# The last block product of a two-level second product: its third column block moved to the end, in two halves

## The chip, the cores and the metric

The kernel runs on one core of one Trainium2 chip. The core has a matrix engine (TensorE, "PE" in the profile, with its weight loads as "PEld"), a vector engine (VectorE, DVE), an activation engine (ScalarE, ACT), a general engine (GpSimd, POOL) and a queue processor for transfers (SyncE, SP). ACT and POOL can issue transfers too. Products are summed in PSUM banks, which VectorE or ScalarE then read; everything else lives in SBUF.

The metric is device microseconds of one execution. A difference of about 0.3% (4.06 us) is what a measurement of this kernel can tell from none.

## The reference

Attention with normalised queries and keys, then a feed-forward block with a squared ReLU. Batch 8, 12 heads, 448 tokens, head size 64; the attention output is laid out as x of 3584 tokens x 768.

```
q_n, k_n = rmsnorm(q, g_q), rmsnorm(k, g_k)
attn = softmax(q_n @ k_n.T / sqrt(64))
x = (attn @ v) as (3584, 768)
h = x @ w_in                 # 768 -> 2048
g = max(h, 0) ** 2
out = g @ w_out              # 2048 -> 768, float32
```

The change touches only the last lines of the work: the product with w_out for the last two batches.

## The kernel before

**Stages.** The tokens are worked through in four spans of two batches (2 x 448 tokens). Attention of the next span runs beside the second product of this one, so that TensorE has matmuls to do while softmax work waits. Both products are block products of the Strassen-Winograd kind: the operands are split in 2 x 2 blocks, seven products of sums of blocks take the place of eight, and adds on VectorE, ScalarE and POOL put the output blocks together. The sums of weight blocks are formed once, early, and kept in device memory (`w2s` for the second product).

**The last span.** Nothing is left to run beside the second product of the last span, so it is done by `last_product` (L1144 to L1318), which divides each of the seven block products again. They are called A11, A12, S2, S1, S3, A22, S4 and are taken in that order by the loop at L1210; `o` counts them and `end` is true for the last, S4. One block product is 384 output columns (three column blocks of 128, numbered m = 0, 1, 2) x 448 tokens, summed over 1024 channels (eight chunks of 128).

Column blocks 0 and 1 are the inner 2 x 2: two column blocks, two halves of the tokens (224 each), two halves of the sum (four chunks each). `run` (L1204) makes one inner product of four matmuls of 128 x 128 by 128 x 224; the trace shows each float32 matmul as two rows, so eight rows. Seven of these follow each other on TensorE: pa (a11 b11), pb (s2 t2), pc (s1 t1), pd (s3 t3), then pa, pd and pc are added to (a12 b21, a22 t4, s4 b22). The inner sums s1 to s4 come from POOL (`add_weights`, L1174) and t1 to t4 from VectorE (`add_g`, L1186); both are formed one block product ahead.

The third column block has no partner. `third` (L1229) computes it directly: eight matmuls of 128 x 448 tokens into one PSUM bank (16 rows in the trace, L1233), then one add of 448 columns on VectorE (L1239). In the order of the program it stands between the first inner product (pa) and the second (pb) of every block product, S4's too.

**PSUM banks.** `bank` gives out two banks in turn ("m" and "n"). Each block product takes two: one for the third column block, one for pc. pa, pb and pd have banks of their own.

**How results leave.** Four of the seven block products finish output blocks (`leaves`). `deliver` (L1137) turns one column block of 128 x 448 on VectorE (a 32 x 32 transpose, L1139) into a buffer of five (`osb`) and sends it with four transfers of 32 rows each (L1142); each piece written to the output is 128 bytes. For most, the transfers all go to SP's queue; blocks 0 and 1 are kept in `late` and delivered at the start of the next block product. For S4 the transfers alternate between SP's queue and ACT's (`queues`, L1225), and blocks 0 and 1 are sent in halves of 224 tokens as they come ready: `send(1, latter)` at L1291, `send(0, former)` at L1301, `send(1, former)` at L1306, `send(0, latter)` at L1311. The third block is sent whole at L1270.

So S4 delivers five times: one whole block (4 transfers of 56 KB) and four halves (16 transfers of 28 KB).

**Order.** The order of instructions on each engine is the order of the program text (the schedule is manual). The layer that builds the program adds waits on semaphores. Transfers issued by SP and ACT share eight completion semaphores, given out in turn in an order that the building layer estimates over both queues. Before an issue, its queue waits until the transfer that had the semaphore before has landed; the queue stands still meanwhile.

**The end.** The whole of this lies in one side of an `If` (L1456; the other side is a kernel for large scores, not run here). Behind the last instruction each engine branches to the common end (L1486), where SP waits for the semaphores of all transfers and the engines meet.

Of the kernel before, what the change touches and what calls it, by code (L numbers as in the profile page):

```python
# [387 lines left out]
def attention_then_ffn_bounded(  # L388
# [35 lines left out]
    nc = tc.nc  # L424

    B, H, S, D = q.shape
# [8 lines left out]
    HC = NPAIR // 2  # L435
    HF = NFC // 2
# [23 lines left out]
    def bank(name, n=None):  # L460

        turn[0] += n is None
        return ps_m.tile([P, S], F32, tag="mn"[turn[0] % 2 if n is None else n], name=name)
# [673 lines left out]
    def deliver(work, span, ct, col, t, queues=(nc.sync,), part=slice(0, S // 32), kept=2):  # L1137
        osb = work.tile([P, S // 32, 32], F32, tag="osb", name="osb", bufs=kept)[:, part]
        nc.vector.transpose(osb.rearrange("p g n -> p (g n)"), ct[:, part.start * 32:part.stop * 32])  # L1139
        for i in range(0, P, 32):  # L1140
            queue = queues[i // 32 % len(queues)]
            queue.dma_start(rows[2 * span + t, :, part, col * P + i:col * P + i + 32], osb[i:i + 32])  # L1142

    def last_product(pool):  # L1144

        rhs_of = {A11: gT[:, 0:HF, 0:S], S2: gC[:, 1], S1: gC[:, 0], S3: gT[:, 0:HF, S:2 * S],
                  A12: gT[:, HF:, 0:S], A22: gC[:, 2], S4: gT[:, HF:, S:2 * S]}
        order = (A11, A12, S2, S1, S3, A22, S4)
        HK, HS = HF // 2, S // 2
# [7 lines left out]
        ts = [[t[:, n * NT2:(n + 1) * NT2].rearrange("p (c n) -> p c n", c=HK) for n in range(4)] for t in (cf, xf)]  # L1157
        dead = [gT[:, f, 0:S] for f in range(HF)] + [gC[:, 1, f] for f in range(HF)]
        late = []
        former, latter = slice(0, HS // 32), slice(HS // 32, S // 32)  # L1160
        sub, add = ALU.subtract, ALU.add

        def weights_of(o, m, k):
            return sets[o % 2].rearrange("p (k c n) -> p k c n", k=2, c=HK)[:, k, :, m * P:(m + 1) * P]

        def sums_of(o):
            return [t.rearrange("p (c n) -> p c n", c=HK) for t in left[o % 2]]
# [6 lines left out]
        def add_weights(o):  # L1174
            if o == len(order):
                return
            s1, s2, s3, s4 = sums_of(o)
            (a11, a12), (a21, a22) = [[weights_of(o, m, k) for k in range(2)] for m in range(2)]
            for dst, x, y, op in ((s1, a21, a22, add), (s2, s1, a11, sub), (s3, a11, a21, sub), (s4, a12, s2, sub)):
                nc.gpsimd.tensor_tensor(dst, x, y, op)  # L1180

        def parts_of(o):
            rhs = rhs_of[order[o]]
            return [[rhs[:, k * HK:(k + 1) * HK, t * HS:(t + 1) * HS] for t in range(2)] for k in range(2)]

        def add_g(o, n):  # L1186
            if o == len(order):
                return
            (b11, b12), (b21, b22) = parts_of(o)
            t1, t2, t3, t4 = ts[o % 2]  # L1190
            dst, x, y = ((t1, b12, b11), (t2, b22, t1), (t3, b22, b12), (t4, b21, t2))[n]
            nc.vector.tensor_tensor(dst, x, y, sub)

        def small_of(name):
            return work.tile([P, HS], F32, tag=name, name=name, bufs=1)
# [8 lines left out]
        def run(ps, lhs, rhs, first=True):  # L1204
            for c in range(HK):
                nc.tensor.matmul(ps, lhs[:, c], rhs[:, c], start=first and c == 0, stop=c == HK - 1,  # L1206
                                 skip_group_check=not first)

        turn[0] += 1
        for o, i in enumerate(order):  # L1210
            end = o + 1 == len(order)
            (b11, b12), (b21, b22) = parts_of(o)
            (a11, a12), (a21, a22) = [[weights_of(o, m, k) for k in range(2)] for m in range(2)]
            s1, s2, s3, s4 = sums_of(o)
            t1, t2, t3, t4 = ts[o % 2]

            into = {A11: [(None, p1s)], A12: [(p1s, None)], S2: [(p1s, p1s)], S1: [(p1s, ys)],
                    S3: [(ys, None), (p1s, p1s)], A22: [(p1s, None)], S4: [(ys, None)]}[i]
            leaves = any(dst is None for _, dst in into)
            into = [(base, dst or homes[i]) for base, dst in into]  # L1220
            at = ((HC if i in (S3, A22) else 0), 1 if i in (S3, S4) else 0)

            def send(m, part=slice(0, S // 32)):
                deliver(work, NSPAN - 1, into[0][1][m], m + at[0], at[1],
                        (nc.sync, nc.scalar) if end else (nc.sync,), part, 5)  # L1225

            both = len(into) > 1

            def third():  # L1229
                m = HC - 1  # L1230
                ps = bank("ps")
                for c in range(HF):
                    nc.tensor.matmul(ps, weights_of(o, m, c // HK)[:, c % HK], rhs_of[i][:, c],  # L1233
                                     start=c == 0, stop=c == HF - 1)
                for base, dst in into:
                    if base is None:
                        nc.scalar.copy(dst[m], ps)
                    else:
                        nc.vector.tensor_tensor(dst[m], base[m], ps, add)  # L1239

            def meet(m, t, left, ps):

                part = slice(t * HS, (t + 1) * HS)
                dst = blocks[m] if both else into[0][1][m]
                nc.vector.tensor_tensor(dst[:, part], left, ps, add)

            def based(m, t, x, name):
                base = into[0][0]
                if both or base is None:
                    return x  # L1250
                y = small_of(name)
                nc.gpsimd.tensor_tensor(y, x, base[m][:, t * HS:(t + 1) * HS], add)
                return y

            def settle(m):
                for base, dst in into if both else ():
                    nc.gpsimd.tensor_tensor(dst[m], base[m], blocks[m], add)

            pa = ps_s.tile([P, 2, 512], F32, tag="s", name="pa")[:, 0, 0:HS]
            run(pa, a11, b11)  # L1260
            p1 = small_of("p1i")
            nc.scalar.copy(p1, pa)
            for n in range(3 if o else 0):
                add_g(o + 1, n)
            for args in late:
                deliver(*args)
            late[:] = []
            third()
            if leaves:
                send(HC - 1)  # L1270
            pb = ps_o.tile([P, S], F32, tag="o", name="pb")[:, 0:HS]
            run(pb, s2, t2)
            z, y = small_of("zi"), small_of("yi")
            nc.vector.tensor_tensor(z, p1, pb, add)
            z21, z12 = based(1, 0, z, "za"), based(0, 1, z, "zb")
            pc = bank("pc")[:, 0:HS]
            run(pc, s1, t1)
            nc.vector.tensor_tensor(y, z, pc, add)
            if o:
                add_g(o + 1, 3)  # L1280
            pd = ps_o.tile([P, S], F32, tag="t", name="pd")[:, 0:HS]
            run(pd, s3, t3)
            add_weights(o + 1)
            if both or into[0][0] is None:
                meet(1, 1, y, pd)
            else:
                meet(1, 1, into[0][0][1][:, HS:S], pd)
                x = into[0][1][1][:, HS:S]
                (nc.vector if end else nc.gpsimd).tensor_tensor(x, x, y, add)
            if end:  # L1290
                send(1, latter)  # L1291
            if o == 0:
                for n in range(4):
                    add_g(1, n)
            run(pa, a12, b21, False)
            if both or into[0][0] is None:
                nc.scalar.copy((blocks if both else into[0][1])[0][:, 0:HS], pa)
            else:
                meet(0, 0, into[0][0][0][:, 0:HS], pa)
            if end:  # L1300
                send(0, former)  # L1301
            run(pd, a22, t4, False)
            meet(1, 0, z21, pd)
            settle(1)
            if end:
                send(1, former)  # L1306
            run(pc, s4, b22, False)
            meet(0, 1, z12, pc)
            settle(0)
            if end:  # L1310
                send(0, latter)  # L1311
            elif leaves:
                for m in (1, 0):
                    late.append((work, NSPAN - 1, into[0][1][m], m + at[0], at[1], (nc.sync,), slice(0, S // 32), 5))
            if o == 0:
                combine(HF - 1)
            load_set(o + 2)
# [173 lines left out]
```

## Time and profile before

| what | us |
|---|---|
| median of 3 runs (1354.04 to 1357.3) | 1354.34 |
| the profiled execution, its own time | 1357.6 |
| its span, first to last instruction | 1355.3 |
| TensorE busy | 1332.5 |
| VectorE, ScalarE, POOL busy | 873.7, 432.1, 619.8 |
| S4's block product on TensorE, from its second product (pb) to its end | 1336.3 to 1345.5 |
| S4's third column block, first row to the next product's first | 6.0 |
| last transpose on VectorE ends | 1346.4 |
| last output transfer issued (SP) | 1350.5 |

The profiled execution took 2.3 us more than its span, and 3.3 us more than the median of the runs. Times in the text are counted from the start of its span.

How to read the views: a row of the timeline has its start, its length, engine, line, operation, what is written and read, shape and count, and in brackets how long the engine was idle before and what ended that. A "q" behind an engine's name means its queue processor: an issue of a transfer, a wait, a branch. A row of the waits has who waited for whom, the sum, the number and the longest. The landing of a transfer is when its semaphore has counted all of its 16 parts.

### The profile page before, as it was taken

To read this page: it belongs to the slowest core of one execution; us is meant where nothing else is said; L and a number is where in the kernel's file an instruction comes from. 1 tells how busy PE (TensorE), PEld (TensorE's weight loads), DVE (VectorE), ACT (ScalarE), POOL (GpSimd) and SP (SyncE) were. 2 spreads that over 40 slices of the span, in tenths; PEclk is the share of its full clock that TensorE was granted. 3 is DMA by queue.
4 is the path that set the end of the run, shared out by engine and by line. 5 is a ranking of instruction groups with operands and counts; after the bars stand their busy time and mean duration, and the time that the engine had idled before them with its cause. 6 is when DMAs were issued, how large, how long until landed. Compare 5 with 4: busy or idle time off the path is not lost.

```text
span 1355.3 us, 17250 instructions
## 1 busy us (share of the span) xinstructions
PE 1332.5 (98%) x5770; PEld 669.6 (49%) x5770; DVE 873.7 (64%) x1537; ACT 432.1 (32%) x681; POOL 619.8 (46%) x504
## 2 busy tenths in 40 slices
PE   8999999999999999999999999999999999999997
PEld 3333445444444455444444455544444445556886
DVE  5999788599987433568777623457878733336552
ACT  7887466533342011233333111223333201111000
POOL 5667533456664122646555212446556412322452
PEclk8999999999999999999999999999999999999999
DMA  9777999655685433345675433345655444431333
GB/s 240 196 244 199 296 364 329 190 126 111 128 160 127 101 87 88 101 111 116 142 147 121 115 96 87 92 109 126 134 120 124 111 100 136 132 88 47 114 106 53
DMA packets 413878, 190.15 MB, mean 140 GB/s; under 512 B 282452, under 2 KB 408788, under 8 KB 413780
## 3 DMA queue, kind: packets, MB, share of 16 engines
q1 hardware_dynamic: 406196, 180.21, 51.8%
q0 software_dynamic: 4736, 8.40, 2.4%
q8 instruction: 48, 0.79, 0.3%
q10 hardware_dynamic: 2848, 0.34, 0.2%
q14 instruction: 50, 0.41, 0.1%
HBM read 155.72 MB, written 33.16 MB: 139 GB/s over the span
## 4 chain that ended last, share of the span: by engine, by line
PE 90%; DVE 5%; ACT 3%; issue 1%; DMA 0%; POOL 0%; DVEq 0%; ACTq 0%
PE ps L1106 29%; PE pd L1068 10%; PE pa L1068 10%; PE pc L1068 10%; PE sc L785 7%; PE pav L862 7%; PE pb L1068 5%; PE ps L1233 3%; PE pd L1206 2%; PE pc L1206 2%; PE pa L1206 2%; ACT gT L797 1%; PE sc L793 1%; DVE gT L810 1%; PE pb L1206 1%
## 5 line engine op out<-in xcount | busy, mean ns | idle before, releaser
L1106 PE MATMUL ps<-gT,sw 128*128 128x448 f32 x576 | 225.8, 543 | 0.0
L1044 POOL TENSOR_TENSOR gT<-gT 128x448 f32<-128x448 f32 x96 | 94.2, 983 | 285.2 <-ACT gT L1040 285.2
L750 POOL TENSOR_TENSOR half<-half,mhalf 128x28 f32<-128x28 f32 x36 | 175.1, 4863 | 74.4 <-DVE half L749 71.2
L1106 PE MATMUL ps<-gC,sw 128*128 128x448 f32 x432 | 170.1, 543 | 0.0
L1106 PEld LDWEIGHTS ps<-gT,sw 128*128 128x128 f32 x576 | 107.5, 190 | 113.9 <-issue 110.4
L1068 PE MATMUL pa<-xT,sw 128*128 128x448 f32 x384 | 155.0, 540 | 0.6 <-ACT p L1072 0.6
L1040 ACT ACTIVATE gT<-gT 128x448 f32<-128x448 f32 x96 | 55.4, 577 | 313.5 <-DVE gT L1083 313.5
L1106 PEld LDWEIGHTS ps<-gC,sw 128*128 128x128 f32 x432 | 80.6, 190 | 86.3 <-issue 84.1
L787 ACT ACTIVATE pr<-sc 128x896 f32<-128x896 f32 x87 | 77.5, 915 | 122.5 <-PE sc L785 122.5
L785 PE MATMUL sc<-qkT 64*64 64x448 f32 (+1 forms) x1152 | 109.8, 496 | 0.0
L1068 PEld LDWEIGHTS pa<-xT,sw 128*128 128x128 f32 x384 | 72.8, 190 | 72.7 <-issue 69.9
L583 POOL TENSOR_TENSOR gC<-gC 128x384 f32<-128x384 f32 x64 | 76.3, 1210 | 62.2 <-DVE gC L579 60.4
L1083 DVE TENSOR_TENSOR gT<-z,pd 128x448 f32<-128x448 f32 x32 | 19.8, 620 | 97.8 <-PE pd L1068 97.6
L1068 PE MATMUL pd<-xT,sw 128*128 128x448 f32 x192 | 77.9, 542 | 1.3 <-DVE z L1075 1.3
L830 POOL DMA_DIRECT2D xT<-factors x72 | 38.1, 534 | 89.1 <-DMA factors<-square 47.9
L1068 PE MATMUL pd<-xC,sw 128*128 128x448 f32 x192 | 77.5, 540 | 1.3 <-DVE gT L1083 1.3
L1068 PE MATMUL pb<-xC,sw 128*128 128x448 f32 x192 | 77.5, 540 | 0.2 <-DVE gT L1083 0.2
L752 POOL TENSOR_TENSOR qk<-qk,half 128x448 f32<-128x448 f32 x72 | 76.2, 1078 | 2.8
L1068 PE MATMUL pc<-xT,sw 128*128 128x448 f32 x192 | 77.4, 539 | 0.0
L1068 PE MATMUL pc<-xC,sw 128*128 128x448 f32 x192 | 77.4, 539 | 0.0
L862 PE MATMUL pav<-pr,vt 64*64 64x448 f32 x348 | 72.7, 537 | 0.0
L862 PE MATMUL rest<-pr,vt 64*64 64x448 f32 x348 | 72.7, 537 | 0.0
(233 smaller groups left out, 2161.0 us busy)
## 6 DMA issues: line engine op xcount, KB each, us to landing
sw<-w1s SPq DMA_DIRECT2D x224, 192.0 KB, 2.4
sw<-w2s SPq DMA_DIRECT2D x126, 256.0 KB, 3.3
w1s<-gC SPq DMA_DIRECT2D x8, 1344.0 KB, 6.6
w2s<-gC SPq DMA_DIRECT2D x8, 1344.0 KB, 6.2
out_dram<-osb SPq DMA_DIRECT2D x182, 56.0 KB, 1.8
qk<-in_q_dram SPq DMA_DIRECT2D x144, 56.0 KB, 3.6
qk<-in_k_dram SPq DMA_DIRECT2D x144, 56.0 KB, 3.0
xT<-factors POOLq DMA_DIRECT2D x72, 112.0 KB, 3.4
```

Of the source, the lines that this page charges most:

```text
L583: nc.gpsimd.tensor_tensor(*[blocks_of(n)[:, place_of(n, i)] for i in (dst, x, y)], op)
L750: nc.gpsimd.tensor_tensor(half, half, mhalf, ALU.pow)
L752: nc.gpsimd.tensor_tensor(qkn[:, s], raw[:, s], half[:, s * NG:(s + 1) * NG].rearrange("p g -> p g ()").to_broadcast([P, NG, 32]), ALU.mult)
L785: nc.tensor.matmul(sc[part, h, 0:n], qkT[rows, 0, 1, keys], qkT[rows, 0, 0, of], start=True, stop=True)
L787: nc.scalar.activation(pr, sc[:, :, 0:n], AF.Exp)
L862: nc.tensor.matmul(into, vs[i][rows, h, c, :], probs[i, c][rows, h, :], start=(c == 0), stop=(c == NF), skip_group_check=True)
L1040: nc.scalar.activation(g, src, AF.Relu)
L1044: nc.gpsimd.tensor_tensor(g, g, g, ALU.mult)
L1068: nc.tensor.matmul(ps, stream[n + at][:, c], rhs[:, c], start=first and c == 0, stop=c == HC - 1, skip_group_check=not first)
L1106: nc.tensor.matmul(ps, stream[n][:, c % 4], rhs_of[i][:, c], start=c == 0, stop=c == HF - 1)
L1206: nc.tensor.matmul(ps, lhs[:, c], rhs[:, c], start=first and c == 0, stop=c == HK - 1, skip_group_check=not first)
L1233: nc.tensor.matmul(ps, weights_of(o, m, c // HK)[:, c % HK], rhs_of[i][:, c], start=c == 0, stop=c == HF - 1)
```

## The change

For S4 alone, the third column block is no longer computed between pa and pb but after all inner products, and in two halves of 224 tokens, each in a bank of its own: eight matmuls of 128 x 224, one add of 224 columns, a transpose and four transfers, twice. Column blocks 0 and 1 of S4 are now sent whole, block 1 after a22 t4 is met and block 0 after s4 b22. S4 thus delivers four times: two whole blocks and two halves, 8 transfers of 56 KB and 8 of 28 KB. The other six block products stay as they were.

```diff
-        former, latter = slice(0, HS // 32), slice(HS // 32, S // 32)
+        halves_of = slice(0, HS), slice(HS, S)
...
             def third():
                 m = HC - 1
-                ps = bank("ps")
-                for c in range(HF):
-                    nc.tensor.matmul(ps, weights_of(o, m, c // HK)[:, c % HK], rhs_of[i][:, c],
-                                     start=c == 0, stop=c == HF - 1)
-                for base, dst in into:
-                    if base is None:
-                        nc.scalar.copy(dst[m], ps)
-                    else:
-                        nc.vector.tensor_tensor(dst[m], base[m], ps, add)
+                for part in halves_of if end else (slice(0, S),):
+                    ps = bank("ps")[:, part]
+                    for c in range(HF):
+                        nc.tensor.matmul(ps, weights_of(o, m, c // HK)[:, c % HK], rhs_of[i][:, c, part],
+                                         start=c == 0, stop=c == HF - 1)
+                    for base, dst in into:
+                        if base is None:
+                            nc.scalar.copy(dst[m][:, part], ps)
+                        else:
+                            nc.vector.tensor_tensor(dst[m][:, part], base[m][:, part], ps, add)
+                    if leaves:
+                        send(m, slice(part.start // 32, part.stop // 32))
...
-            third()
-            if leaves:
-                send(HC - 1)
+            if not end:
+                third()
             pb = ps_o.tile([P, S], F32, tag="o", name="pb")[:, 0:HS]
...
-            if end:
-                send(1, latter)
...
-            if end:
-                send(0, former)
             run(pd, a22, t4, False)
             meet(1, 0, z21, pd)
             settle(1)
             if end:
-                send(1, former)
+                send(1)
             run(pc, s4, b22, False)
             meet(0, 1, z12, pc)
             settle(0)
             if end:
-                send(0, latter)
+                send(0)
+                third()
```

## The prediction

> **What bounds the kernel now.** The page first: TensorE is busy for 98% of the span and makes 90% of the chain that ended last, so the body is matmul time, and outside it only the ends of the program are left to win or lose.
>
> ```profile
> span 1355.3 us, 17250 instructions
> ...
> PE 1332.5 (98%) x5770; PEld 669.6 (49%) x5770; DVE 873.7 (64%) x1537; ACT 432.1 (32%) x681; POOL 619.8 (46%) x504
> ...
> PE 90%; DVE 5%; ACT 3%; issue 1%; DMA 0%; POOL 0%; DVEq 0%; ACTq 0%
> ```
>
> Next the timeline of the last 14 us (start, length, engine, line, operation). TensorE's last product ends at 1343.82 + 1.68 = 1345.50 and VectorE's last transpose at 1346.44, yet the span ends at 1355.3. So 8.9 us hold no computation, only the output transfers of line 1142 and the program's end.
>
> ```profile
> 1342.29 5.78 ACTq L1142 DMA_DIRECT2D out_dram<-osb  x8
> ...
> 1343.82 1.68 PE L1206 MATMUL pc<-gT,qkT 128*128 128x224 f32 x8
> ...
> 1345.30 5.65 SPq L1142 DMA_DIRECT2D out_dram<-osb  x8
> 1345.61 0.39 DVE L1245 TENSOR_TENSOR gT<-zb,pc 128x224 f32<-128x224 f32 x1 [0.68 <-PE pc L1206]
> 1346.03 0.41 DVE L1139 STREAM_TRANSPOSE osb<-gT 128x224 f32<-128x224 f32 x1
> ```
>
> Then the waits of SP's queue from 1336 on, and single issues from narrow windows of the timeline. SP waits 10.4 us for other transfers to land and makes its last two issues at 1349.84 and 1350.50, 4 us after the data were ready. The pair at 1346.68 (SP) and 1346.83 (ACT) is slow to issue: 1.39 and 1.24 us where its neighbours take 0.32 to 0.46, both ending near 1348.07.
>
> ```profile
> SPq L1142 <- DMA out_dram<-osb: 10.4, 3, 4.9
> ...
> 1346.68 1.39 SPq L1142 DMA_DIRECT2D out_dram<-osb  x1
> ...
> 1346.83 1.24 ACTq L1142 DMA_DIRECT2D out_dram<-osb  x1
> ...
> 1349.84 1.11 SPq L1142 DMA_DIRECT2D out_dram<-osb  x2
> ```
>
> Last, by line, the branch out of the program's `If` (L1456) and the first instruction behind it (L1486), with first and last start. SP leaves at 1351.0 and goes on at 1353.6; ACT leaves at 1348.1 and goes on at 1350.7. So the branch costs 2.6 us on either, and SP's is the one that ends the program: 1350.95 (end of its last issue) + 0.1 + 2.6 + 1.65 (its closing waits and the barrier) = 1355.3.
>
> ```profile
> L1456 SPq COMPARE_BRANCH  x1: 43/43/43, 1351.0 to 1351.0; - x1
> ...
> L1486 SPq EVENT_SEMAPHORE  x14: 17/28/28, 1353.6 to 1355.2; - x14
> ...
> L1456 ACTq COMPARE_BRANCH  x1: 38/38/38, 1348.1 to 1348.1; - x1
> ...
> L1486 ACTq DRAIN  x2: 8/44/81, 1350.7 to 1354.7; - x2
> ```
>
> Why is SP late? Transfers of SP and ACT take eight completion semaphores in turn, and an issue first waits until the semaphore's former user has landed. In the built program most of SP's last transfers follow the ACT transfer of the same delivery: SP's issue at 1345.30 came when ACT's of 1342.29 had landed (1345.24), that of 1348.93 when ACT's of 1345.14 had landed (1348.87), that of 1349.34 after 1345.59's (1349.32). Those landings take 3 to 3.7 us: 15 of 16 parts arrive 1.4 us after the issue, the last one up to 2.3 us behind them, around two instruction fetches of 16 KB (records of queue 8 at 1342.91 and 1346.72; I take them for TensorE's, since its branch begins at 1342.0).
>
> **The change, part by part.** Times are those of the profiled execution.
>
> 1. *TensorE, third block moved.* It leaves the place between pa and pb, where its 16 rows of 448 columns take 6.01 us, and everything behind comes 6.02 us earlier (pb starts at 1330.24 in place of 1336.26). At the end stand 32 rows of 224 columns. Neighbouring products of that shape take 1.51 us for 8, so 32 take 6.04. The last matmul ends at 1345.50 + 0.03 = 1345.53. The 16 extra weight loads are priced at nothing: in those rows each load (0.190) lies under the matmul before it. Were they all exposed, 16 x 0.190 = 3.0 us; a gain is excluded, no multiply goes. I take 0.03, from rows of the very shape.
>
>    The Trainium skill, "TensorE: Matmul & The Clock Gate", part "The mechanism" on packing, says that a weight load overlaps running matmuls only when the row group differs. These loads use the whole array, so by it each would be exposed, and a gain of 2.9 us would go to those 3.0. The rows above are full-array loads too, back to back at 0.189 us a pair, so the measurement decides against it here.
>
> 2. *Cover lost behind pa.* The block hid other engines' work. In the new order: POOL's s3 and s4 for the last block end at 1326.70 + 2.51 = 1329.2, pd wants them at 1333.2. VectorE's two late transposes end at 1331.03, its z add is due at 1332.0. ACT's copy of pa ends at 1330.8. pc uses the bank emptied at 1320.5, the first half that emptied at 1329.4, the second half that of pc, read until 1340.0 and wanted at 1342.1. SP's eight late issues end at 1334.7, the first new one is due at 1339.2. All have over 1 us to spare except z (1.0), and z is next needed by y at 1333.5. Cost 0; each would begin to cost when late by its margin.
>
> 3. *VectorE at the end.* The last piece is again an add (0.39) and a transpose (0.41) of 224 columns after a TensorE end, so its data are ready at 1346.47, against 1346.44. Two transposes of 0.645 and two of 0.41 stand where there were one and four, the others mid-stream. Cost 0.03, the same as in 1.
>
> 4. *Transfers.* Before, the last block issues 4 of 56 KB and 16 of 28 KB on two queues; after, 8 and 8: four issues fewer, same bytes. Column block 1 is ready at 1339.15, block 0 at 1340.65, the halves at 1343.4 and 1346.47. Each gives two issues per queue. Before, twelve issues stood behind 1343 on VectorE's side; now eight do, spread over 3 us.
>
> 5. *The semaphore waits on SP's queue.* In the new built program, SP's second issue of block 0 waits for ACT's second of block 0 (issued 1341.1, landed 1342.9 at 1.8 us, or 1345.2 if the fetch at 1342.91 catches its last part); behind it stand both halves. SP's second of the first half waits for ACT's first of that half (issued 1343.44; landing at 1345.1 with the smallest delay in the trace, 1.7, or 1347.2 with the largest, 3.7). SP's second of the last half waits for ACT's second of the first half (1343.8 plus the same: 1345.5 to 1347.5). Between these I take 2.3, SP's median for that size, which is clear of VectorE's 1346.47. So SP's last two issues start at 1346.48 and 1346.84.
>
> 6. *The end.* The last issue takes 0.45 (done 1347.3) or is as slow as those before it (done 1348.07). TensorE's second fetch comes with its branch, which is not moved, and the last issue falls at the very time of the two slow ones, so I take 1348.07. The end is then 1348.07 + 0.1 + 2.6 + 1.65 = 1352.4, a gain of 2.9; without the stall 1351.6, a gain of 3.7. The late landing of the last parts (1348.75 plus 0.2 for each transfer behind the fetch, five of them: 1349.8) stays under SP's return at 1350.75. With 3.7 us landings in step 5, SP's second of the first half goes at 1347.2, the last at 1348.0 to 1348.5: end 1352.8, a gain of 2.4.
>
>    The Trainium skill, "DMA: Bandwidth & Descriptors", gives a transfer about 2.0 us plus bytes over 436 GB/s. By it, as an estimate, 28 KB land after 2.1 us, SP never waits and the gain would be the 3.7; it has no word for the last of sixteen parts that this trace shows arriving 2 us late.
>
> Sum: +0.03 for TensorE, -2.9 at the tail, -2.9 us in all. The profiled execution took 1357.6 us, 2.3 beyond its span and 3.3 over the median of the runs; nothing shows where those 3.3 lie, so I take the difference off the median: 1354.34 - 2.9 = 1351.4, or -0.21%. 0.3%, about what a measurement of this kernel can tell from no change, is 4.06 us.
>
> **Rivals.**
>
> *B, the tail clears fully.* No slow issue (gain 3.7), and the return from the branch shorter because fewer output packets share the engines with its fetch. The transfers move in 2 us stretches at a busy share of 0.33 to 0.60 while the branches are fetched; a return in 2.1 in place of 2.6 gives 4.2: 1350.1. Against it: ACT's return took the same 2.6 with much traffic as SP's with little.
>
> *C, a new wait replaces the old.* ACT's half-transfers land only when the fetch at 1346.72 is through, as those of 1345.14 did at 1348.87. Then SP's second of the first half goes at 1348.9, the last at 1349.6 to 1350.05: end 1354.4, gain 0.9, 1353.4. Against it: they are issued 1.7 us earlier, and only the fetch at 1342.91 lies in their way, whose victims landed by 1345.73.
>
> *D, the weight loads show, and it is slower.* If in the direct halves no load overlapped, 32 x 0.190 = 6.1 us would come on the path: +6.1 - 2.9, or 1357.5. It decides from 0.09 us a load (2.9/32). For it: the same 16 weights are loaded once more. Against it: step 1's rows.
>
> **How the numbers follow.** My case 0.60, B 0.23, C 0.10, D 0.07. Runs of this kernel lie up to 3.3 us apart (1354.04 to 1357.3), so I move 0.05 of my case beyond the 4.06 us and leave 0.02 of D within. Faster 0.23 + 0.05 = 0.28; slower 0.05; same 0.67. My case alone: 1350.6 to 1352.0. The range takes in B at its better end (4.7, all returns short) and C with 1 us of scatter: 1349.6 to 1354.4.
>
> **What would show it.** Right: TensorE's last row ends within 0.1 of where it did; the 224-column rows of the third block keep 0.189 us; SP's waits for transfers fall well below 10.4; its last issue ends at 1347.3 to 1348.1 on the old scale, and 4.3 us later the span ends. Wrong: gaps between those rows (D), an SP issue after 1349 (C), a stall of TensorE behind pa (step 2), or an end set by an engine other than SP or ACT.

## The result, and the profile after

The changed kernel takes 0.9979 of the time of the kernel before, with a 95% interval of 0.9972 to 0.9987. The medians of 20 runs each are 1353.51 us and 1355.79 us. The forecast was 1351.4 us and -0.21%; the time lies in its range (1349.6 to 1354.4), and the change lies within the 0.3% that it called "same".

The page of the kernel after, the lines that answer to those of before:

```profile
span 1350.1 us, 17275 instructions
...
PE 1329.7 (98%) x5786; PEld 671.6 (50%) x5786; DVE 873.4 (65%) x1537; ACT 431.8 (32%) x681; POOL 619.4 (46%) x504
```

The span is 5.2 us shorter, more than the times allow. Half of it isn't the change: TensorE's first row of the first product (`pa`) comes at 134.87 before and 132.28 after, and the 2.59 us stay to the end (last useful row done at 1345.50 and 1342.91). That part is taken up in the last section. So the tails are compared here: from the end of TensorE's last useful row to the end of the span. It is 1355.27 - 1345.50 = 9.77 us before and 1350.08 - 1342.91 = 7.17 us after, 2.60 us less.

The last pieces of the chain that ended last, kernel after (start, length, what):

```profile
1333.83 1.51 PE pd L1206 x8
1335.34 1.51 PE pc L1206 x8
1336.85 6.07 PE ps L1234 x32
1342.92 0.02 issue
1342.94 0.40 DVE gT L1240
1343.34 0.02 issue
1343.37 0.41 DVE osb L1139
```

The two halves follow the inner products without a gap, 32 rows in 6.07 us, against 16 rows in 6.01. VectorE's last add and transpose are as long as before.

Now SP's waits from 1333 on, kernel after (sum, number, longest):

```profile
SPq L1142 <- DVE osb L1139: 5.4, 3, 4.4
SPq L1142 <- DMA out_dram<-osb: 3.3, 2, 2.5
```

Single issues from narrow windows of its timeline:

```profile
1343.81 0.32 SPq L1142 DMA_DIRECT2D out_dram<-osb  x1
...
1344.16 1.38 SPq L1142 DMA_DIRECT2D out_dram<-osb  x1
...
1344.22 1.32 ACTq L1142 DMA_DIRECT2D out_dram<-osb  x1
```

And the branch (here L1455) with what follows it (L1485), by line, with first and last start:

```profile
L1455 SPq COMPARE_BRANCH  x1: 43/43/43, 1345.6 to 1345.6; - x1
...
L1485 SPq EVENT_SEMAPHORE  x14: 17/28/28, 1348.4 to 1350.0; - x14
...
L1455 ACTq COMPARE_BRANCH  x1: 38/38/38, 1345.6 to 1345.6; - x1
...
L1485 ACTq DRAIN  x2: 8/44/80, 1348.2 to 1349.5; - x2
```

SP now waits mostly for data (VectorE's transposes), no longer mostly for landings: 3.3 us in place of 10.4. Its last issue starts at 1344.16, 1.25 us after TensorE's last row; before it started 5.0 us after. The second issue of each queue is still slow, and SP and ACT now leave by the branch together.

### The profile page after: what moved, and what is told of

It is laid out like the page before. It is cut to its first block, busy times and chain, and to the rows that moved or that the text cites. A ratio compares the mean times of both kernels' runs of the same rounds, so it can differ in the third digit from the quotient of the medians.

```text
span 1350.1 us, 17275 instructions
## 1 busy us (share of the span) xinstructions
PE 1329.7 (98%) x5786; PEld 671.6 (50%) x5786; DVE 873.4 (65%) x1537; ACT 431.8 (32%) x681; POOL 619.4 (46%) x504
## 4 chain that ended last, share of the span: by engine, by line
PE 89%; DVE 5%; ACT 2%; DMA 1%; issue 1%; POOL 0%; SPq 0%; POOLq 0%; DVEq 0%
PE ps L1106 29%; PE pd L1068 10%; PE pa L1068 10%; PE pc L1068 10%; PE sc L785 7%; PE pav L862 7%; PE pb L1068 5%; PE ps L1234 3%; PE pd L1206 2%; PE pc L1206 2%; PE pa L1206 2%; DVE gT L810 1%; PE pb L1206 1%; DVE rstd L715 1%; ACT gT L797 1%
```

## The experiments

The theory was that the tail is set by SP's last issue, the branch and the closing waits, and that the change pays by having fewer output issues in line. The rivals were that the move of the third block pays, that the halves pay, or that the waits across the two queues do. All tails below are from the end of the last useful row.

| kernel | third block | blocks 0 and 1 sent | issues | last issue done, us after the last row | tail, us | ratio to before (95%) |
|---|---|---|---|---|---|---|
| before | early | in halves | 20 | 5.4 | 9.77 | |
| the change | last, two halves | whole | 16 | 2.6 | 7.17 | 0.9979 (0.9972 to 0.9987) |
| last, one piece | last, whole | whole | 12 | 2.5 | 7.26 | 0.9979 (0.9969 to 0.9988) |
| early, sent whole | early | whole | 12 | 2.4 | 7.11 | 0.9978 (0.9967 to 0.9988) |
| last, sent in halves | last, two halves | in halves | 24 | 3.8 | 8.08 | 0.9989 (0.9980 to 0.9998) |
| before, SP alone | early | in halves | 20 on one queue | 6.7 | 10.98 | 1.0015 (1.0006 to 1.0024) |
| the change, SP alone | last, two halves | whole | 16 on one queue | 3.8 | 8.15 | 0.9984 (0.9975 to 0.9993) |

Each tail is that of one profiled execution, so tails 0.1 us apart can't be told from each other here. The ratios come from 8 to 20 runs of each kernel, each set against runs of the kernel before taken beside it; they fall in the same groups as the tails.

**The third block last, in one piece.**

```diff
-                for part in halves_of if end else (slice(0, S),):
+                for part in (slice(0, S),):
```

> The changed kernel with S4's third column block last but in one piece of 448 columns, in one bank, sent whole. The measure is the tail: from the end of TensorE's last row to the end of the span, 9.8 us before (1345.50 to 1355.27) and 7.2 us with the change (1342.92 to 1350.08). Theory (the end is set by SP's last issue, the branch and the closing waits, and that issue is held until TensorE's fetch is over, 2.6 us after its last row): the data are ready 1.4 us after the last row in place of 0.9, still under those 2.6, so the tail stays at 7.2 to 7.5 and the time at -0.15% to -0.25% against before. Rival (the halves pay, since they shorten the last add and transpose by 0.5 us): the tail is 7.7, half a microsecond of the gain gone.

The tail is 7.26 us, as the theory had it, but not for its reason. VectorE needs 0.62 + 0.65 us in place of 0.39 + 0.41 behind the last row, and the queues' second issues are done 2.45 us after that row, against 2.63 with the change. The theory had them held by TensorE's second fetch (queue 8). Here that fetch starts 1.95 us before the last row, at 1343.55, and an earlier issue of SP is the slow one. The last block's second issue takes 0.72 us with no such fetch beside it (the fetch record from a narrow window of the transfers: packets, MB, share; then two single issues):

```profile
q8 instruction: 1, 0.02, 87.4%
...
1343.77 1.60 SPq L1142 DMA_DIRECT2D out_dram<-osb  x1
...
1347.23 0.72 SPq L1142 DMA_DIRECT2D out_dram<-osb  x1
```

So the data come later, their issues are shorter, and the return from the branch is longer (3.1 us for SP, against 2.84): that the sum is the same is in part luck. As built, the split into halves can't be told from nothing (0.09 us).

**The third block early, the other two sent whole.** This is the kernel before with nothing moved on TensorE.

```diff
-            if end:
-                send(1, latter)
...
-            if end:
-                send(0, former)
...
-                send(1, former)
+                send(1)
...
-                send(0, latter)
+                send(0)
```

> The kernel before, third column block between pa and pb as it was, but blocks 0 and 1 of S4 sent whole (12 issues in place of 20). Theory (the gain comes from fewer output issues behind each other on SP's queue, with no wait for ACT's transfers just issued): the tail falls from 9.8 to 7.2 to 7.5, the time by 0.17% to 0.2% against before, though nothing on TensorE is moved. Rival (the move of the third block to the end pays, as it spreads the transfers): the tail stays near 9.8, no change in time.

The tail is 7.11 us, a little under the expected 7.2 to 7.5, and the ratio 0.9978: the whole gain of the change, without the change that gives it its name. The waits of SP's queue from 1333 on have no transfer left in them, only data and the program's end:

```profile
SPq L1142 <- DVE osb L1139: 9.9, 3, 6.5
SPq L1482 <- PEq L1482: 0.7, 2, 0.5
```

And its last issues, from narrow windows of the timeline, lie where the data are (the last transpose ends at 1346.16):

```profile
1346.18 0.32 SPq L1142 DMA_DIRECT2D out_dram<-osb  x1
...
1346.54 0.88 SPq L1142 DMA_DIRECT2D out_dram<-osb  x1
...
1346.60 0.82 ACTq L1142 DMA_DIRECT2D out_dram<-osb  x1
```

So the rival, by which the gain needs the move, falls. What the change takes away that counts is the sending of blocks 0 and 1 in four halves. That doesn't show what the move does while the halves stay; the next experiment does.

**The third block last, but blocks 0 and 1 sent in halves.** The four `send` calls in halves are put back in the changed kernel.

```diff
+        former, latter = slice(0, HS // 32), slice(HS // 32, S // 32)
...
+            if end:
+                send(1, latter)
...
+            if end:
+                send(0, former)
...
-                send(1)
+                send(1, former)
...
-                send(0)
+                send(0, latter)
```

> The changed kernel, with blocks 0 and 1 of S4 still sent in halves as before (24 issues in place of 16). Theory: the third block's 6 us behind the inner products give SP's queue time to catch up; worked through the semaphore waits, its last two issues come at 0.9 and 1.3 us after TensorE's last row, so the tail is 7.2 to 8.0. Rival (the number of issues alone sets the tail): with four more issues than before, 9.8 or more, and no gain.

The tail is 8.08 us, just over the expected 7.2 to 8.0, and 1.7 us under the kernel before in spite of four more issues. So the number of issues alone doesn't set the tail; their time before the end counts too, and the move does pay 1.7 us where the halves stay. What was mis-sized: SP was to have caught up by the last half. It hadn't. Its slow issue (1.42 us, at 1.40 after the last row) was the first half's second, and the last half's two came at 2.92 and 3.35. SP waited 8.7 us for landings (its waits from 1333 on):

```profile
SPq L1142 <- DMA out_dram<-osb: 8.7, 6, 4.7
```

**One queue alone, before and after.** The same edit in both kernels:

```diff
-                        (nc.sync, nc.scalar) if end else (nc.sync,), part, 5)
+                        (nc.sync,), part, 5)
```

> The kernel before with all of S4's transfers on SP's queue, so that no SP issue waits for an ACT transfer just issued. Theory (the tail is a matter of issues in line): 16 issues of about 0.5 us from 3.2 us before TensorE's last row, with two stretches held by fetches, put the last one at 4.9 to 6.0 us behind it; tail 9.3 to 10.4, no gain. Rival (only the waits across the two queues make the tail long): tail near 7.5, 0.17% faster than before.

> The changed kernel with all of S4's transfers on SP's queue. Theory: the last half's four issues stand in line (start 0.9 us after TensorE's last row, the second held until 2.6, two more of 0.45), so SP's last issue ends at 3.6, the tail is 8.0 to 8.6 against 7.2, and about 1 us of the gain goes. Rival (with few issues the second queue is of no use): 7.2.

In the kernel before, the waits across queues are gone with this (SP's waits list no landing at all from 1334 on), and the tail grows to 10.98 us. The line itself is too long: 16 issues from 3.2 us before the last row to 6.7 us after it, two of them slow (1.52 and 1.59 us), the rest 0.32 to 0.50. The expected 9.3 to 10.4 was short by 0.6 us, since the last issue was done at 6.72 (it started at 6.28), not by 6.0.

The timeline of the kernel before on SP alone, its 16 half transfers in one stretch and the last data:

```profile
1339.49 9.93 SPq L1142 DMA_DIRECT2D out_dram<-osb  x16
...
1343.23 0.41 DVE L1139 STREAM_TRANSPOSE osb<-gT 128x224 f32<-128x224 f32 x1
```

The last transfer's data are there at 1343.64, and the line runs on to 1349.42.

So the rival falls that only those waits make the tail long. But the edit takes the waits away and doubles SP's line at once, so it doesn't price the waits of two queues. They did hold SP in the kernel before: of the first half block that was ready, ACT issued its first transfer at 1342.29 and SP its own at 1345.30, when that one had landed. Two queues that share no semaphores were not tried, so how the 2.7 us of gain with fewer issues divide between shorter lines and fewer waits stays open. In the changed kernel the same edit costs 1.0 us of tail (8.15), as expected: the second queue halves the last half's four issues.

**Six more matmuls behind the last useful one.**

```diff
                 send(0)
                 third()
+                spin = ps_s.tile([P, 2, 512], F32, tag="s", name="spin")[:, 0, 0:S]
+                for c in range(6):
+                    nc.tensor.matmul(spin, weights_of(o, 0, 0)[:, c % HK], rhs_of[i][:, c], start=c == 0, stop=c == 5)
```

> The changed kernel with six more matmuls of 448 columns (4.5 us) behind the last useful one, into a bank that nobody reads; TensorE's branch and its two fetches come 4.5 us later. They are work that the reference doesn't ask for. Tails are counted from the last useful row. Theory (the slow second issues of SP and ACT, 1.38 and 1.32 us, come from TensorE's fetch behind its branch): both take about 0.45, SP's last issue ends at 1.7 to 1.8 in place of 2.6, and the tail is 6.2 to 6.5 in place of 7.2 although TensorE ends later. Rival (the slow issues come from the output transfers themselves, or from VectorE's fetch): they stay at 1.2 to 1.4, and the tail at 7.2 or more.

Timeline of that kernel (the single issues from narrow windows):

```profile
1344.80 0.92 PE L1234 MATMUL ps<-gT,qk 128*128 128x224 f32 x4
1345.56 4.67 PE L1313 MATMUL spin<-gT,qk 128*128 128x448 f32 x12
...
1346.18 0.41 DVE L1139 STREAM_TRANSPOSE osb<-gT 128x224 f32<-128x224 f32 x1
...
1347.14 0.76 SPq L1142 DMA_DIRECT2D out_dram<-osb  x1
...
1347.04 0.46 ACTq L1142 DMA_DIRECT2D out_dram<-osb  x1
```

The fetch records of queue 8, taken for TensorE's, from narrow windows: the changed kernel's second one (it starts at 1343.95), then this kernel's (1348.85):

```profile
q8 instruction: 1, 0.02, 73.0%
```

```profile
q8 instruction: 1, 0.02, 93.0%
```

TensorE works 4.5 us longer, and the program ends earlier after its last useful row (1344.80 + 0.92 = 1345.72): 1352.24 - 1345.72 = 6.52 us in place of 7.17, just over the expected 6.2 to 6.5. ACT's second issue takes 0.46 in place of 1.32, SP's 0.76 in place of 1.38, so SP's last issue is done at 2.2 us and not by 1.8. The second fetch, 1.0 us after the last useful row in the changed kernel, now comes 3.1 us after it (2.1 us later, not the 4.5 expected). So the slow issues do come from that fetch, as far as ACT's shows. Of SP's 0.9 us above its usual 0.45, 0.3 remain. Another fetch, of 8 KB on queue 14, starts at 1347.23, inside that issue; the slow 0.72 us of the kernel with the third block in one piece has one beside it too, also at 1347.23. That speaks for the rival's fetch by another engine as the cause of this rest, but no run tests it. The ratio to before, 0.9982 (0.9972 to 0.9991), can't tell this from the change itself: 0.65 us is 0.05%.

**Without the branch.**

```diff
-    with tc.If(bits <= limit) as small_scores:
-        with tc.manual_schedule():
-            attention_then_ffn_bounded(tc, *args, held)
-    with small_scores.Else():
-        attention_then_ffn_with_row_max(tc, *args)
+    with tc.manual_schedule():
+        attention_then_ffn_bounded(tc, *args, held)
```

> The changed kernel without its If: the choice between the two kernels and the whole kernel for large scores are left out; the value that it decides by is still loaded. No engine branches at the end. Theory (2.6 to 2.8 us of the tail are the return from the branch, and the slow issues its fetch): SP's last issue ends at 1.8 after TensorE's last row, its closing waits follow at once and wait for the last landing near 3.5, and the tail is 5.0 to 5.7; the time at least 0.1% below the changed kernel's, and more if the start gains too. Rival (the end waits for landings or the engines' meeting whatever the branch): tail 6.5 to 7.2.

The tail is 4.19 us, less than the expected 5.0 to 5.7 and 3.0 us under the change's. There is no fetch at the end, both second issues are usual (0.45 and 0.46 us), and SP's closing waits begin 1.8 us after the last row, at once behind its last issue:

```profile
L1482 SPq EVENT_SEMAPHORE  x14: 17/28/28, 1349.4 to 1351.7; - x14
```

They then wait for landings (the last at 1350.71). So the branch with what it brings, fetches and return, is 3 us of the tail. The total shows none of it, where at least 0.1% less than the change was expected: the ratio to before is 0.9979 (0.9969 to 0.9988), that of the change. TensorE's last row ends at 1347.61, and the first scores start at 10.78 us in place of 8.88: without the branch VectorE's scaling of the first pair (L339) stands behind a reduction of the next (it starts at 8.24, against 6.70 in the changed kernel). That is 1.5 of the 1.9 us lost there; the other 0.4 are TensorE's transposes behind it (L380), 0.98 us in place of 0.57 in a stretch of half clock. That order came with the edit; it wasn't tested by itself.

**Two of the last transfers on POOL's queue.**

```diff
-                        (nc.sync, nc.scalar) if end else (nc.sync,), part, 5)
+                        (nc.sync, nc.scalar, nc.gpsimd, nc.gpsimd) if end and part.start else (nc.sync, nc.scalar) if end else (nc.sync,), part, 5)
```

> The changed kernel, but the second half of the third block is sent by three queues: one transfer by SP, one by ACT, two by POOL, which has been idle for 12 us. Theory: SP and ACT are done 1.25 us after TensorE's last row, before the fetch holds them, and return from the branch at 4.0 to 4.3; POOL's two issues of 0.53 land after 3.4 us (its figure elsewhere in the profile), near 5.0, and the closing waits follow: tail 6.2 to 6.7, half a microsecond to one better than the change. Rival (POOL's transfers start or land later than SP's): tail 7.2 or more.

The worst run of all: 1.0041 (1.0029 to 1.0054), tail 15.56 us where 6.2 to 6.7 were expected. The issues went nearly as expected: SP and ACT one each, done 1.3 us after the last row, and POOL's two (0.67 and 0.60 us) landed 4.7 us after it at the latest, 0.7 us behind the others. SP and ACT returned from the branch at 4.9 and 4.8 us, not at 4.0 to 4.3: it took them 3.6 and 3.5 us. None of this makes the tail. POOL ends the program with a drain of its own behind the branch, and this takes 9.3 us in the changed kernel and 9.5 us here. POOL's instructions behind the branch, first in the changed kernel, then in this one (duration in ns min/median/max, then first and last start):

```profile
L1485 POOLq DRAIN  x3: 40/107/9297, 1332.5 to 1349.8; - x3
```

```profile
L1485 POOLq DRAIN  x3: 40/107/9456, 1349.4 to 1359.4; - x3
```

In the changed kernel POOL leaves 13 us before the last row and its drain is over before anyone waits. Here it starts at 1349.4, 5.0 us after the last row, and the end waits for it.

## Why the prediction was right, point by point

**Step 1, TensorE.** Right. 32 rows took 6.07 us (6.04 forecast, 6.01 the old form): the 16 extra weight loads lie under the matmuls. The rule cited from the Trainium skill ("TensorE: Matmul & The Clock Gate", "The mechanism"), by which they would show, would have made it about 9 us (an estimate: 6.04 + 3.0); the measurement decides against it for these full-array loads, as the rows of before had. The same part also lets a load of the background weight buffer go ahead of running matmuls, so the page as a whole doesn't demand those 3 us.

**Step 2, the cover lost behind pa.** Right: no gap on TensorE from pa to the end, each product 1.51 us.

**Step 3, VectorE.** Right: data ready 0.87 us after the last row, 0.94 before.

**Steps 4 and 5, issues and waits.** Right, and close in time. Counted from TensorE's last row, SP's second issue of the first half was forecast at 0.22 us and came at 0.13; the last two at 0.95 and 1.31, and came at 0.90 and 1.25. SP's second issue of block 0 did wait for ACT's second of block 0, and as long as 2.5 us, since that landed 2.36 us after its issue and not 1.8. It cost nothing, as the last half's data came later. The 2.0 us plus bytes over 436 GB/s that step 6 cites from the Trainium skill ("DMA: Bandwidth & Descriptors", "Anatomy of one DMA — SWDGE (gpsimd) path") are fitted there to transfers issued by GpSimd. The 28 KB transfers of SP and ACT whose landing the profile after shows took 2.2 to 3.2 us, all more than the 2.1 estimated by it.

**Step 6, the end.** The slow last issue was kept, rightly: 1.38 us, done 2.63 us after the last row (2.54 forecast). The return from the branch was the term mis-sized: 2.6 us were taken, 2.84 were measured, and 3.0 to 3.1 in the two kernels with 12 issues, where SP and ACT likewise leave together. With both in turn before, each took 2.6. That they share something there is a match over these runs; no run tests it. Hence a tail gain of 2.60 us in place of 2.9, and -0.21% (-0.13% to -0.28%, or 1.8 to 3.8 us) by the times.

**The sum and the rivals.** The change of -0.21% was forecast and measured; that the last digit agrees is luck, since the tail fell by 0.3 us less than forecast and the interval is 2 us wide. The absolute 1351.4 was 2.1 us too low, mostly as the median of three runs that it started from, 1354.34, was 1.45 us below the median of twenty. B failed on both its parts: the slow issues stayed and the return grew. C failed: ACT's first transfer of the first half landed 2.2 us after its issue, where 3.7 us and a wait for the second fetch were feared. D failed with step 1.

**What the prediction didn't say.** It gave the tail's gain as one sum, with the fewer issues and the move of the third block in it together, and didn't ask whether the move is needed. The experiment with the third block early shows that it isn't. Either remedy shortens the tail by itself: fewer issues (9.77 to 7.11), or more time behind the many issues (9.77 to 8.08). Together they give no more than the better one. In all three kernels with fewer issues on two queues the last issue is done at 2.4 to 2.6 us, and the branch and the closing waits take the rest; only the edits that touch the fetch or the branch went lower (6.52 and 4.19).

## What to carry to other kernels

A finer cut of the last results makes the data ready earlier and can end the program later: count the issues that still stand in line when the last data are ready, on each queue, with its waits for semaphores shared with the other queue. When the last compute is done microseconds before the span ends, follow the queue processors through their last issue, the branch and the closing waits; what ends last there decides which edit can pay. Here, once the issues no longer stood in line, the tail stayed at 7.1 to 7.3 us until the fetch or the branch itself was moved. An idle engine with a transfer queue isn't free help at the end, if it has closing work of its own.

## What the runs showed of the hardware that was not expected

POOL's closing drain takes 9.3 us behind the branch in the eight profiles with a branch where adds were POOL's last work, 9.5 in the one where transfers were, and 10.6 without the branch. It shows in the time only in the one where POOL was late; in the others it was over before SP's closing waits.

The granted clock of TensorE fell to half for 3.4 us at a time (6.8 once) at the start of eight of the ten profiled executions, and those end later. Windows of the start, kernel before and kernel after (length, then busy time of TensorE, its weight loads, VectorE, ACT and POOL, granted clock, share and rate of transfers):

```profile
9.00:13.00 4.00, 4.00 (x14) 1.83 (x16) 1.52 (x4) 3.14 (x6) 2.61 (x2) 0.57 0.80 226
...
22.00:27.00 5.00, 4.41 (x16) 1.82 (x18) 4.70 (x10) 3.29 (x8) 1.23 (x1) 0.66 1.11 324
```

```profile
9.00:13.00 4.00, 3.91 (x20) 1.52 (x20) 1.58 (x4) 3.97 (x8) 2.55 (x2) 1.00 0.84 224
...
22.00:27.00 5.00, 5.00 (x29) 1.94 (x29) 4.38 (x10) 3.65 (x8) 1.20 (x2) 1.00 1.12 324
```

Of the ten profiles, the two with no such stretch (the change; the kernel before on SP alone) have the last useful row done at 1342.9 and 1342.7 us, three with one stretch at 1344.4 to 1345.5, and the four with two and a branch at 1345.5 to 1345.8. That fits the 3 to 5 us by which runs of one kernel differ (1354.04 to 1359.18 before). The twelve runs with the six added matmuls fit too: the five with a mean granted clock of 1.0 took 1351.82 to 1352.69 us, the seven with 0.997 to 0.999 took 1353.9 to 1356.15. It is a match, not a test: nothing here changed the clock on purpose. It is also the reason why tails were compared, and not spans.
